# A gated linear attention and an MLP in one kernel: from a scheduler's order to a hand-written two-phase pipeline with head pairs, casting DMAs and a crossbar transpose

## The chip, the core and the metric

The kernel runs on one core of a Trainium2 chip. The core has TensorE (PE, matmuls, with its own weight loads, PEld), VectorE (DVE), ScalarE (ACT), GpSimd (POOL) and SyncE (SP). DMAs are issued here by POOL and by SP and run on 16 DMA engines. The metric is the device time of one execution, in microseconds.

## What is computed

```python
def _attn_ref(q, k, v, alpha):                 # all (4, 8, 768, 48) float32
    state = zeros((B, H, D, D)); y = zeros_like(q)
    for t in range(S):
        state = alpha[:, :, t, :, None] * state + einsum('bhd,bhe->bhde', k[:, :, t], v[:, :, t])
        y[:, :, t] = einsum('bhd,bhde->bhe', q[:, :, t], state)
    return y
def _moe_ref(x, w_in, w_out):                  # x (3072, 384), w_in (384, 2048), w_out (2048, 384)
    return gelu_tanh(x @ w_in) @ w_out
x = attn.transpose(0, 2, 1, 3).reshape(B * S, H * D)   # the heads side by side
```

Both kernels cut the 768 steps into 6 chunks of 128. Inside a chunk the decay is carried by cumulative sums of ln(alpha): with b = exp(cumulative sum), q is multiplied by b and k by 1/b, so that the chunk becomes plain attention with a mask, q' k'^T masked times v, plus q' times the state of the chunk before. The state then is (state + k'^T v) times the decay of the whole chunk. The 24 units (6 chunks x 4 batch elements) of 128 rows go through the MLP in groups of the four units of a chunk.

## The kernel before, in words

A framework schedules the program: the code below is written unit by unit, and the order on each engine is chosen by the framework from tile pools and dependences.

Front. For pairs of units alpha is loaded by POOL (L105), ln is taken on ACT (L108), and PE sums it along the rows with an upper triangular matrix (L114) and with one column sum per head (L118). DVE stores the sums (L120), and ACT takes exp of the column sums (L121). This is done for all 24 units before anything else of them. SP loads w_in (L93) and w_out (L130) as float32, and DVE casts them (L127, L159).

Rear. Three stages are staggered by one unit each. Stage a loads q, k, v (L190, POOL). Stage b takes exp of the sums with both signs (L200, L202), multiplies q and k (L205, L206), casts v (L208), transposes q and k head by head on PE (L213, L214) and copies them out of PSUM (L215 on ACT, L216 on DVE). Stage c makes the scores (L234), masks them (L237), and then y from scores and v (L241) and from q and the state (L243), and k^T v (L245); DVE updates the state (L249, L250), ACT casts y to `x_sb` (L255), PE transposes it (L259) and DVE copies it (L260).

The MLP of a group is cut into pieces: 16 of layer 1 (three matmuls L275 and a gelu L279) and 4 of layer 2 (16 matmuls L286, copy L291, store L293 on SP). Up to seven waiting pieces are put behind each stage c.

ACT has tables for sets of functions; ACT_TABLE_LOAD rows at lines L108, L121, L200, L202 and L279 are changes between them.

Of the kernel before, what the change touches and what calls it, by code (L numbers as in the profile page):

```python
# [3 lines left out]

# [6 lines left out]
BF16 = mybir.dt.bfloat16  # L12
F32 = mybir.dt.float32
AF = mybir.ActivationFunctionType
ALU = mybir.AluOpType

MU = -0.1074356


@with_exitstack  # L20
def kernel(
    ctx: ExitStack,
    tc: tile.TileContext,
    q: bass.AP,
    k: bass.AP,
    v: bass.AP,
    alpha: bass.AP,
    moe_w_in: bass.AP,
    moe_w_out: bass.AP,
    out: bass.AP,  # L30
):
    nc = tc.nc
    B, H, S, D = q.shape
    C = 128
    NCH = S // C
    NT = B * NCH
    d_model = moe_w_in.shape[0]
    d_ff = moe_w_in.shape[1]
    NKT = d_model // C
    NFT = d_ff // C  # L40

    const = ctx.enter_context(tc.tile_pool(name="const", bufs=1))
    glob = ctx.enter_context(tc.tile_pool(name="glob", bufs=1))

    ut = const.tile([C, C], BF16)
    make_upper_triangular(nc, ut, val=1.0, diag=True)
    ones_col = const.tile([C, 1], BF16)
    nc.vector.memset(ones_col, 1.0)
    iota_i = const.tile([C, 1], mybir.dt.int32)
    nc.gpsimd.iota(iota_i, pattern=[[1, 1]], base=1, channel_multiplier=1)  # L50
    bias_pos = const.tile([C, 1], F32)
    nc.vector.tensor_single_scalar(bias_pos, iota_i, MU, op=ALU.mult)
    bias_neg = const.tile([C, 1], F32)
    nc.vector.tensor_single_scalar(bias_neg, iota_i, -MU, op=ALU.mult)
    bias_end = const.tile([C, 1], F32)
    nc.vector.memset(bias_end, C * MU)
    mu_row_i = const.tile([1, C], mybir.dt.int32)
    nc.gpsimd.iota(mu_row_i, pattern=[[1, C]], base=1, channel_multiplier=0)
    mu_row = const.tile([1, C], BF16)
    nc.vector.tensor_single_scalar(mu_row, mu_row_i, MU, op=ALU.mult)  # L60
    ones_row = const.tile([1, H * D], BF16)
    nc.vector.memset(ones_row, 1.0)

    xT_all = glob.tile([C, NKT, NT, C], BF16)
    states = []
    for b in range(B):
        st = glob.tile([C, H, D], BF16, name=f"state_b{b}")
        nc.vector.memset(st, 0.0)
        states.append(st)
    cum_all = glob.tile([C, NT, H * D], mybir.dt.float16)  # L70
    bend_all = glob.tile([D, NT, H], F32)
    w_in_sb = glob.tile([C, NKT, d_ff], BF16)
    w_out_sb = glob.tile([C, NFT, d_model], BF16)
    NRING = 4
    qp_ring = [glob.tile([C, H, 64], BF16, name=f"qp_ring{i}") for i in range(NRING)]
    kp_ring = [glob.tile([C, H, 64], BF16, name=f"kp_ring{i}") for i in range(NRING)]
    for t_ in qp_ring + kp_ring:
        nc.gpsimd.memset(t_[:, :, D:64], 0.0)
    qT_ring = [glob.tile([C, H, C], BF16, name=f"qT_ring{i}") for i in range(NRING)]
    kT_ring = [glob.tile([C, H, C], BF16, name=f"kT_ring{i}") for i in range(NRING)]  # L80
    for t_ in qT_ring + kT_ring:
        nc.vector.memset(t_[64:, :, :], 0.0)
    ident = const.tile([C, C], BF16)
    from concourse.masks import make_identity
    make_identity(nc, ident)

    units = [(c, b) for c in range(NCH) for b in range(B)]

    if True:
        wstage = ctx.enter_context(tc.tile_pool(name="wstage", bufs=1))  # L90
        w_in_f32 = wstage.tile([C, NKT, d_ff], F32, tag="stage")
        for j in range(NKT):
            nc.sync.dma_start(  # L93
                w_in_f32[:, j, :], moe_w_in.rearrange("(j c) n -> c j n", c=C)[:, j, :]
            )

        psb = ctx.enter_context(tc.tile_pool(name="psb", bufs=1, space=bass.MemoryType.PSUM))
        with tc.tile_pool(name="wka", bufs=int(os.environ.get("GLA_WKA_BUFS", 5))) as wka:
            for pi in range(0, len(units), 2):
                pair = units[pi:pi + 2]  # L100
                NP2 = len(pair)
                a8 = wka.tile([C, NP2, H, D], F32, tag="a8")
                for i, (c, b) in enumerate(pair):
                    tsl = slice(c * C, (c + 1) * C)
                    nc.gpsimd.dma_start(  # L105
                        a8[:, i], alpha[b].rearrange("h s d -> s h d")[tsl])
                la8 = wka.tile([C, NP2, H, D], BF16, tag="la8")
                nc.scalar.activation(la8, a8, AF.Ln, scale=float(math.exp(-MU)))  # L108
                tts = [b * NCH + c for (c, b) in pair]
                for i, (c, b) in enumerate(pair):  # L110
                    tt = tts[i]
                    bank = psb.tile([C, H * D + H], F32, tag="hT", bufs=int(os.environ.get("MOE_HT_BUFS", 2)), name="cumla")
                    cumla, ce_i = bank[:, 0:H * D], bank[0:D, H * D:]
                    nc.tensor.matmul(cumla, ut,  # L114
                                     la8[:, i].rearrange("t h d -> t (h d)"),
                                     start=True, stop=True)
                    for h in range(H):
                        nc.tensor.matmul(ce_i[:, h:h + 1], la8[:, i, h, :],  # L118
                                         ones_col, start=True, stop=True)
                    nc.vector.tensor_copy(cum_all[:, tt, :], cumla)  # L120
                    nc.scalar.activation(bend_all[:, tt, :], ce_i, AF.Exp,  # L121
                                         bias=bias_end[0:D, 0:1], scale=1.0)

        w_out_f32 = wstage.tile([C, NFT, d_model], F32, tag="stage")
        for piece in range(8):
            psl = slice(piece * (d_ff // 8), (piece + 1) * (d_ff // 8))
            nc.vector.tensor_copy(w_in_sb[:, :, psl], w_in_f32[:, :, psl])  # L127
        for j in range(4):
            sl = slice(j * (NFT // 4), (j + 1) * (NFT // 4))
            nc.sync.dma_start(  # L130
                w_out_f32[:, sl, :],
                moe_w_out.rearrange("(n c) p -> c n p", c=C)[:, sl, :],
            )

    work = ctx.enter_context(
        tc.tile_pool(name="work", bufs=int(os.environ.get("GLA_WORK_BUFS", 4))))
    trans = ctx.enter_context(
        tc.tile_pool(name="trans", bufs=int(os.environ.get("GLA_TRANS_BUFS", 3))))
    moe = ctx.enter_context(tc.tile_pool(name="moe", bufs=2))
    args = dict(B=B, H=H, S=S, D=D, C=C, NCH=NCH, NKT=NKT, NFT=NFT,  # L140
                d_model=d_model, d_ff=d_ff, NT=NT)
    live = {}
    NU = len(units)
    GRP = B
    pending = []
    for step in range(NU + 2):
        if step < NU:
            live[step] = _gla_stage_a(nc, work, q, k, v, units[step], **args)
        if 1 <= step <= NU:
            u = step - 1  # L150
            _gla_stage_b(nc, work, trans, psb, ident, live[u], units[u],
                         cum_all, bias_pos, bias_neg,
                         qp_ring[u % NRING], kp_ring[u % NRING],
                         qT_ring[u % NRING], kT_ring[u % NRING], **args)
            if u < 4:
                for piece in (2 * u, 2 * u + 1):
                    psl = slice(piece * (NFT // 8) * d_model,
                                (piece + 1) * (NFT // 8) * d_model)
                    nc.vector.tensor_copy(  # L159
                        w_out_sb.rearrange("c n p -> c (n p)")[:, psl],  # L160
                        w_out_f32.rearrange("c n p -> c (n p)")[:, psl],
                    )
        if 2 <= step:
            u = step - 2
            c, b = units[u]
            _gla_stage_c(nc, work, psb, ident, live.pop(u), units[u],
                         ut, bend_all, states[b], xT_all, **args)
            if not int(os.environ.get("GLA_SEQ_MOE", 0)):
                take = min(int(os.environ.get("MOE_PIECES", 7)),
                           max(0, len(pending) - int(os.environ.get("MOE_RESERVE", 0))))  # L170
                for _ in range(take):
                    pending.pop(0)()
# [6 lines left out]
    while pending:  # L179
        pending.pop(0)()  # L180
# [150 lines left out]
```

## Time and profile before

| | us |
|---|---|
| median of 3 runs (lowest, highest) | 298.85 (297.84, 299.3) |
| span of the profiled execution, first to last instruction | 295.8 |
| of the median outside this span | 3.05 |
| PE / ACT / DVE / POOL busy in the span | 224.5 / 200.8 / 141.3 / 87.4 |
| PE busy in 0 to 74 us, 74 to 122, 122 to 296 | 21.0, 40.6, 162.9 |

The profile gives no other time of the profiled execution than its span; what lies around it is taken from the runs. Busy times of engines overlap, so they do not add to the span. The last line is the one to start from: PE is nearly idle in the first quarter and nearly full in the rest.

### The profile page before, as it was taken

What the parts mean: (1) busy time and instruction counts of PE and PEld (TensorE: products, weight loads), DVE (VectorE), ACT (ScalarE), POOL (GpSimd) and SP (SyncE); (2) the same over time, 40 slices, a digit from 0 to 9 for tenths busy, and PEclk for the clock granted to TensorE, in tenths of its full rate; (3) what the DMA queues carried; (4) which work ended last, traced back from release to release, by engine and by line L of the source; (5) the groups of instructions that cost most, each with busy time, mean ns of one, the idle gap of its engine ahead of it and who ended that gap; (6) DMA issues with size and microseconds to landing.
All of it is one profiled execution on the core that took longest, in us unless ns stands there. A gap on an engine that the chain in (4) does not pass through costs nothing.

```text
span 295.8 us, 5241 instructions
## 1 busy us (share of the span) xinstructions
PE 224.5 (76%) x2112; PEld 132.8 (45%) x2112; DVE 141.3 (48%) x274; ACT 200.8 (68%) x301; POOL 87.4 (30%) x114
## 2 busy tenths in 40 slices
PE   0043333332778989899998999999999999999983
PEld 0022212221656535556556555565456644554441
DVE  7183433222599855567548144656243633540011
ACT  0257787978677999996999999945761276304800
POOL 9643321005988758153333213220000000000000
PEclk9999999999999999999999999999999999999999
DMA  7999951002999979373232512241001100011011
GB/s 278 283 187 274 291 126 53 0 1 67 193 187 187 189 144 198 89 181 99 80 82 59 182 53 55 53 109 53 2 1 55 53 2 0 3 53 55 0 53 54
DMA packets 12168, 30.22 MB, mean 102 GB/s; under 512 B 2032, under 2 KB 7152, under 8 KB 11760
## 3 DMA queue, kind: packets, MB, share of 16 engines
q0 software_dynamic: 6144, 18.88, 30.4%
q1 hardware_dynamic: 6000, 11.01, 11.0%
q8 instruction: 16, 0.26, 0.4%
q14 instruction: 8, 0.07, 0.1%
HBM read 25.17 MB, written 4.72 MB: 101 GB/s over the span
## 4 chain that ended last, share of the span: by engine, by line
PE 47%; ACT 34%; DMA 7%; DVE 6%; issue 3%; POOL 1%; SPq 0%; DVEq 0%; POOLq 0%; ACTq 0%
PE acc L286 16%; PE hT L275 15%; ACT gT L279 6%; ACT L279 5%; ACT L108 4%; DMA w_in_f<-in_moe_w_in_dram 4%; ACT qT_ring L215 3%; PE kT_ps L214 3%; PE qT_ps L213 3%; ACT la L108 3%; PE at_ps L234 2%; ACT L200 2%; ACT L202 2%; ACT L121 2%; DVE w_in_sb L127 2%
## 5 line engine op out<-in xcount | busy, mean ns | idle before, releaser
L275 PE MATMUL hT<-xT_all,w_in_sb 128*128 128x512 bf16 x288 | 74.5, 379 | 4.0 <-ACT gT L279 3.8
L286 PE MATMUL acc<-w_out_sb,gT 128*128 128x384 bf16 x384 | 70.8, 326 | 3.0 <-DVE ot L291 2.8
L279 ACT ACTIVATE gT<-hT 128x512 bf16<-128x512 f32 x96 | 55.5, 598 | 16.3 <-PE hT L275 14.2
L286 PEld LDWEIGHTS <-gT 128*128 128x128 bf16 x384 | 36.4, 97 | 28.0 <-issue 4.0
L114 PE MATMUL cumla<-la,ut 128*128 128x384 bf16 x24 | 11.6, 485 | 48.3 <-ACT la L108 39.1
L291 DVE COPY ot<-acc 128x384 f32<-128x384 f32 x24 | 13.3, 555 | 53.6 <-PE acc L286 53.6
L237 DVE TENSOR_TENSOR atm<-at_ps,ut 128x512 bf16<-128x512 f32 x48 | 31.1, 683 | 15.9 <-PE at_ps L234 15.7
L275 PEld LDWEIGHTS <-w_in_sb 128*128 128x128 bf16 x288 | 24.8, 97 | 26.3 <-issue 5.5
L118 PEld LDWEIGHTS <-la 128*48 128x48 bf16 x192 | 9.5, 129 | 55.5 <-issue 55.5
L190 POOL DMA_DIRECT2D q<-in_q_dram x24 | 21.2, 884 | 44.1 <-PE cumla L118 24.1
L120 DVE CAST cum_all<-cumla 128x384 f16<-128x384 f32 x24 | 13.3, 556 | 32.5 <-PE cumla L118 32.5
L190 POOL DMA_DIRECT2D v<-in_v_dram x24 | 21.2, 885 | 25.3 <-ACT v8b L208 21.8
L105 POOL DMA_DIRECT2D a<-in_alpha_dram x24 | 21.5, 900 | 21.3 <-ACT la L108 18.9
L215 ACT COPY qT_ring<-qT_ps 64x1024 bf16<-64x1024 bf16 x24 | 24.1, 1005 | 4.9 <-PE qT_ps L213 4.6
L190 POOL DMA_DIRECT2D k<-in_k_dram x24 | 21.2, 885 | 18.3 <-DVE kp_ring L206 17.4
L208 ACT CAST v8b<-v 128x384 bf16<-128x384 f32 x24 | 12.3, 512 | 18.7 <-PE yps L243 17.9
L216 DVE COPY kT_ring<-kT_ps 64x1024 bf16<-64x1024 bf16 x24 | 16.3, 680 | 17.5 <-PE kT_ps L214 17.1
L108 ACT ACT_TABLE_LOAD x11 | 14.1, 1283 | 13.4 <-DMA a<-in_alpha_dram 13.2
L213 PE MATMUL qT_ps<-ident,qp_ring 128*64 128x128 bf16 x192 | 18.3, 230 | 5.9 <-DVE qp_ring L205 5.3
L205 DVE TENSOR_TENSOR qp_ring<-q,b 128x384 bf16<-128x384 f32 x24 | 13.2, 551 | 14.6 <-PE at_ps L234 5.7
L213 PEld LDWEIGHTS <-qp_ring 128*64 128x64 bf16 x192 | 12.7, 114 | 16.5 <-issue 14.9
L255 ACT CAST x_sb<-yps 128x384 bf16<-128x384 f32 x24 | 11.4, 476 | 12.7 <-PE yps L243 10.6
(49 smaller groups left out, 319.2 us busy)
## 6 DMA issues: line engine op xcount, KB each, us to landing
a<-in_alpha_dram POOLq DMA_DIRECT2D x24, 192.0 KB, 7.2
q<-in_q_dram POOLq DMA_DIRECT2D x24, 192.0 KB, 5.3
k<-in_k_dram POOLq DMA_DIRECT2D x24, 192.0 KB, 5.7
v<-in_v_dram POOLq DMA_DIRECT2D x24, 192.0 KB, 5.2
out_dram<-ot SPq DMA_DIRECT2D x24, 192.0 KB, 1.9
w_in_f<-in_moe_w_in_dram SPq DMA_DIRECT2D x3, 1024.0 KB, 7.4
w_out_f<-in_moe_w_out_dram SPq DMA_DIRECT2D x4, 768.0 KB, 12.4
```

Of the source, the lines that this page charges most:

```text
L105: nc.gpsimd.dma_start(a8[:, i], alpha[b].rearrange("h s d -> s h d")[tsl])
L108: nc.scalar.activation(la8, a8, AF.Ln, scale=float(math.exp(-MU)))
L120: nc.vector.tensor_copy(cum_all[:, tt, :], cumla)
L190: nc.gpsimd.dma_start(t_sb, t_dram[b].rearrange("h s d -> s h d")[tsl])
L213: nc.tensor.transpose(qT_ps[:, h, :], qp[:, h, :], ident)
L215: nc.scalar.copy(qT[0:64], qT_ps)
L216: nc.vector.tensor_copy(kT[0:64], kT_ps)
L237: nc.vector.tensor_tensor(atm, at_ps, ut[:, None, :].to_broadcast([C, 4, C]), op=ALU.mult)
L275: nc.tensor.matmul(hT, w_in_sb[:, j, nt * C:(nt + 1) * C], xsl, start=(j == 0), stop=(j == NKT - 1),)
L279: nc.scalar.activation(gT[:, nt, :], hT, AF.Gelu_apprx_tanh)
L286: nc.tensor.matmul(acc, gT[:, nt, mt * C:(mt + 1) * C], w_out_sb[:, nt, :], start=(nt == 0), stop=(nt == NFT - 1),)
L291: nc.vector.tensor_copy(ot, acc)
```

## The change

The program is written anew, under a manual order: each engine runs its instructions in the order in which the code issues them.

- Heads are kept in pairs, padded from 48 to 64 columns each, so that a pair is 128 wide. q and k are transposed on PE a pair at a time. The scores of the two heads of a pair are matmuls on 64 rows each, on the upper and the lower half of the array, into two PSUM banks. kv and the state are made for a pair at once; the state tile is zero off the diagonal blocks.
- The state has two tiles per batch element, used in turn; in chunk 0 there is no state term, in the last chunk no kv.
- ln and exp use one table set, which is loaded by hand, and there is no stored cumulative sum: exp is taken from PSUM in the phase before the unit is used.
- Two phases per group. Layer 2 of the group before runs with, merged into it, the kv and y of this group's units and ln, sums and exp of the next group. Layer 1 of this group runs with the transposes and scores of the next group.
- v, w_in and w_out are cast to bf16 by the DMA, all on POOL's queue. q, k and alpha of chunks 0 and 1 are loaded by SP, those of later chunks by POOL.
- x goes from ACT's cast to `xT` by a DMA transpose on SP's queue, where the stores are too.

```diff
-                nc.gpsimd.dma_start(a8[:, i], alpha[b].rearrange("h s d -> s h d")[tsl])
-    for t_dram, t_sb in ((q, q8), (k, k8), (v, v8)):
-        nc.gpsimd.dma_start(t_sb, t_dram[b].rearrange("h s d -> s h d")[tsl])
+    def load(self, names, pair, eng):
+        for n in names:
+            dt = F32 if n != "v" else BF16
+            t = self.ld.tile([self.C, 2, self.H, self.D], dt, tag=n + "8", bufs=6 if n == "v" else 4, name=n + "8")
...
+                e = eng if n != "v" else self.nc.gpsimd
+                e.dma_start(t[:, i], self.src[n][b].rearrange("h s d -> s h d")[sl])
...
+            ps = self.ps.tile([C, 2, H // 2, C], BF16, tag="yk", bufs=2, name="qkT_ps")
+            for j, s in enumerate((u["qp"], u["kp"])):
+                for p in range(H // 2):
+                    nc.tensor.transpose(
+                        ps[:, j, p, :], s[:, 2 * p:2 * p + 2, :].rearrange("t h d -> t (h d)"), self.ident)
+            nc.vector.tensor_copy(t, ps)
...
+        at = self.ps.tile([C, 2, H // 2, C], F32, tag="ca", name="at")
+        for p in range(H // 2):
+            for o in range(2):
+                sl = slice(64 * o, 64 * o + 64)
+                nc.tensor.matmul(at[:, o, p, :], kT[sl, p, :], qT[sl, p, :], start=True, stop=True)
...
+        x = self.wk.tile([C, H * D], BF16, tag="x", name="x")
+        nc.scalar.copy(x, yps.rearrange("t h d -> t (h d)"))
+        if DMA_X:
+            nc.sync.dma_start_transpose(xT[:, :, i, :], x)
...
+        for p in pairs[0]:
+            self.load("aqk", p, nc.sync)
...
+        for p in pairs[1]:
+            self.load("a", p, nc.sync)
+        for i in range(4):
+            self.load_w_in(i, 4)
+        for p in pairs[1]:
+            self.load("qk", p, nc.sync)
+            self.load("v", p, nc.gpsimd)
...
+                if g + 2 < len(G):
+                    side.append(lambda: [self.load("aqkv", p, nc.gpsimd) for p in pairs[g + 2]])
+                ln, cum, exp = decays(pairs[g + 1])
+                side += [lambda: self.act_set(LN_EXP_SET), ln[0]]
+                side += [lambda: self.yk(G[g][0], xT, 0), ln[1]]
+                side += [lambda: self.yk(G[g][1], xT, 1), cum[0], exp[0]]
+                side += [lambda: self.yk(G[g][2], xT, 2)]
+                side += [lambda: self.yk(G[g][3], xT, 3), cum[1], exp[1]]
...
+            main = self.layer2(G[g - 1], gT_prev) if g else []
+            _merge(main, side, 0.0, 0.8)
...
+                    side.append(lambda cb=cb: self.attn(cb))
+            _merge(self.layer1(xT, gT), side, 0.1, 1.0)
```

`_merge` spreads the side items evenly over the stated part of the main pieces; layer 1 has 16 pieces of three matmuls, layer 2 has 16 of four.

Where instructions stand. First DVE in the rear of the kernel before (`qp_ring`, `kp_ring` are q and k after the decay, `kT_ring` the transposed k):

```order
L206 TENSOR_TENSOR kp_ring_100<-k_817,binv_908 128x8x48
L237 TENSOR_TENSOR atm<-at_ps,ut 128x512 x2
L216 COPY kT_ring_116<-kT_ps 64x1024
L249 TENSOR_TENSOR stmp<-kv,state_b_83 48x384
L205 TENSOR_TENSOR qp_ring_97<-q_901,b_1026 128x8x48
L250 TENSOR_TENSOR state_b_83<-stmp,bend_all 48x384
L206 TENSOR_TENSOR kp_ring_101<-k_902,binv_1027 128x8x48
L260 COPY xT_all<-xT_ps 128x3x128
```

Then DVE now, from the states of chunk 0 to the first scores of chunk 1 (`q_166`, `k_169` are chunk 1's first pair of units, `q_175`, `k_178` its second; `qkT` is transposed q and k):

```order
L202 TENSOR_TENSOR st_1_94<-kv,bend 64x4x48 x2
L145 TENSOR_TENSOR qp_105<-q_166,b_394 128x16x48
L147 TENSOR_TENSOR kp_109<-k_169,binv_395 128x16x48
L202 TENSOR_TENSOR st_1_96<-kv,bend 64x4x48 x2
L202 TENSOR_TENSOR st_1_98<-kv,bend 64x4x48 x2
L145 TENSOR_TENSOR qp_106<-q_175,b_451 128x16x48
L147 TENSOR_TENSOR kp_110<-k_178,binv_452 128x16x48
L166 COPY qkT<-qkT_ps 128x1024
L180 TENSOR_TENSOR atm<-at,ut 128x512 x2
```

Before, units were staggered singly and each product stood near the work of its own unit; now both products of chunk 1 stand ahead of the first copy that layer 1's merged score matmuls need, with the state updates of chunk 0 between them.

SP before, all of it:

```order
L93 DMA w_in_f_135<-in_moe_w_in_dram 128x2048 x3
L130 DMA w_out_f_494<-in_moe_w_out_dram 128x4x384 x4
L293 DMA out_dram<-ot 128x384 x24
```

SP now, its start (`a_112` to `k_127` are chunk 0, `a_156` to `k_178` chunk 1):

```order
L93 DMA q_124<-in_q_dram 128x8x48 x2
L93 DMA k_127<-in_k_dram 128x8x48 x2
L93 DMA a_156<-in_alpha_dram 128x8x48 x2
L93 DMA a_159<-in_alpha_dram 128x8x48 x2
L93 DMA q_166<-in_q_dram 128x8x48 x2
L93 DMA k_169<-in_k_dram 128x8x48 x2
L93 DMA q_175<-in_q_dram 128x8x48 x2
L93 DMA k_178<-in_k_dram 128x8x48 x2
L221 DMA_TRANSPOSE xT<-x 128x3x128 x4
L258 DMA out_dram<-ot 128x384
```

POOL now, the same time (`v_172`, `v_181` are chunk 1, `a_318` to `v_339` chunk 2, `a_642` chunk 3):

```order
L100 DMA w_in<-in_moe_w_in_dram 128x3x512 x4
L93 DMA v_172<-in_v_dram 128x8x48 x2
L93 DMA v_181<-in_v_dram 128x8x48 x2
L93 DMA a_318<-in_alpha_dram 128x8x48 x2
L93 DMA q_321<-in_q_dram 128x8x48 x2
L93 DMA k_336<-in_k_dram 128x8x48 x2
L93 DMA v_339<-in_v_dram 128x8x48 x2
L106 DMA w_out<-in_moe_w_out_dram 128x4x384 x4
L93 DMA a_642<-in_alpha_dram 128x8x48 x2
```

SP had the weights and the stores; now it has 24 loads of a, q and k, then transposes and stores. POOL had all loads of a, q, k, v; now it has the weights among them.

## Rows read from the trace of the kernel before

**Rows 1.** The page, busy time and share of the span, PE
```profile
PE 224.5 (76%) x2112; PEld 132.8 (45%) x2112; DVE 141.3 (48%) x274; ACT 200.8 (68%) x301; POOL 87.4 (30%) x114
```

**Rows 2.** Busy us (count) of PE, PEld, DVE, ACT, POOL; clock, DMA share, GB/s
```profile
0.00:74.00 74.00, 21.04 (x216) 12.03 (x216) 29.15 (x59) 48.32 (x66) 28.03 (x47) 1.00 0.59 156
...
122.00:296.00 174.00, 162.87 (x1403) 93.77 (x1402) 76.23 (x146) 110.79 (x171) 23.85 (x27) 1.00 0.20 59
```

**Rows 3.** Chain of waits, the front: start us, us, what
```profile
1.65 11.86 DMA w_in_f<-in_moe_w_in_dram
13.64 6.05 DVE w_in_sb L127 x8
20.93 1.28 ACT L108
...
72.55 4.38 DMA q<-in_q_dram
```

**Rows 4.** Chain of waits, dense pieces of the rear
```profile
156.18 0.56 PE qT_ps L213 x8
...
196.62 2.60 PE acc L286 x16
...
278.20 1.33 PE hT L275 x6
```

**Rows 5.** Timeline of PE: start us, us, engine, line, operation, tiles, count
```profile
15.83 0.48 PE L118 MATMUL cumla<-ones_col,la 128*48 128x1 bf16 x8
16.24 0.50 PE L114 MATMUL cumla<-la,ut 128*128 128x384 bf16 x1
...
155.29 0.20 PE L241 MATMUL yps<-v8b,atm 128*128 128x48 bf16 x1
...
155.69 0.18 PE L243 MATMUL yps<-state_b,qT_ring 128*128 128x48 bf16 x1
```

**Rows 6.** Busy time where only w_in, w_out, and q, k, v move
```profile
3.00:6.00 3.00, 0.00 (x0) 0.00 (x0) 2.62 (x9) 0.00 (x0) 2.99 (x5) 1.00 1.02 418
25.80:27.40 1.60, 0.62 (x9) 0.50 (x9) 0.93 (x2) 1.18 (x2) 0.00 (x0) 1.00 1.07 373
86.00:96.00 10.00, 7.74 (x123) 6.07 (x124) 9.73 (x21) 7.24 (x13) 8.39 (x11) 1.00 1.05 189
```

**Rows 7.** Tiles out_dram, then w_out_f: issue to landing
```profile
DMA to landing us min/median/max: 1.8/1.9/5.0
...
DMA to landing us min/median/max: 7.8/12.4/17.0
```

**Rows 8.** The page, DMA queues: POOL's, SP's
```profile
q0 software_dynamic: 6144, 18.88, 30.4%
q1 hardware_dynamic: 6000, 11.01, 11.0%
```

**Rows 9.** Groups by line and shape: busy us, mean ns | idle before
```profile
L279 ACT ACTIVATE gT<-hT 128x512 bf16<-128x512 f32 x96 | 55.5, 598 | 16.3 <-PE hT L275 14.2
L237 DVE TENSOR_TENSOR atm<-at_ps,ut 128x512 bf16<-128x512 f32 x48 | 31.1, 683 | 15.9 <-PE at_ps L234 15.7
L279 ACT ACT_TABLE_LOAD x14 | 18.0, 1283 | 0.3
L216 DVE COPY kT_ring<-kT_ps 64x1024 bf16<-64x1024 bf16 x24 | 16.3, 680 | 17.5 <-PE kT_ps L214 17.1
...
L205 DVE TENSOR_TENSOR qp_ring<-q,b 128x384 bf16<-128x384 f32 x24 | 13.2, 551 | 14.6 <-PE at_ps L234 5.7 <-DMA q<-in_q_dram 5.2 <-PE qT_ps L213 1.1
...
L250 DVE TENSOR_TENSOR state_b<-stmp,bend_all 48x384 bf16<-48x384 f32 x24 | 13.1, 544 | 1.1 <-PE yps L243 1.0
...
L255 ACT CAST x_sb<-yps 128x384 bf16<-128x384 f32 x24 | 11.4, 476 | 12.7 <-PE yps L243 10.6 <-PE hT L275 2.0
L108 ACT ACTIVATE la<-a 128x768 bf16<-128x768 f32 x12 | 10.0, 841 | 0.1
...
L202 ACT ACT_TABLE_LOAD x6 | 7.7, 1283 | 0.1
```

**Rows 10.** Chain of waits, its last piece
```profile
292.07 0.56 DVE ot L291
```

More of the change, by code (lines that the diff above doesn't have):

```diff
@@ L2 @@
-import math
-import os
-from contextlib import ExitStack
 import concourse.bass as bass
@@ L8 @@
 from concourse import mybir
-from concourse._compat import with_exitstack
-from concourse.masks import make_upper_triangular
+from concourse.masks import make_identity, make_upper_triangular
 BF16 = mybir.dt.bfloat16
+F16 = mybir.dt.float16
 F32 = mybir.dt.float32
@@ L15 @@
 ALU = mybir.AluOpType
[L17 to L172, printed above, removed]
-            if u % GRP == GRP - 1:
-                tts = [units[uu][1] * NCH + units[uu][0]
-                       for uu in range(u - GRP + 1, u + 1)]
-                pending.extend(
-                    _moe_pieces(nc, moe, psb, xT_all, w_in_sb, w_out_sb, out,
-                                tts, **args))
-    while pending:
-        pending.pop(0)()
@@ L220, in _gla_stage_c @@
-def _gla_stage_c(nc, work, psb, ident, live, unit, ut, bend_all, state, xT_all,
-                 *, H, D, C, NCH, NKT, **_):
-    c, b = unit
-    tt = b * NCH + c
-    qT, kT, kp, v8b = live["qT"], live["kT"], live["kp"], live["v8b"]
-    yps = psb.tile([C, H, D], F32, tag="ybank",
-                   bufs=int(os.environ.get("GLA_Y_BUFS", 1)))
-    kv = psb.tile([D, H, D], F32, tag="kv", bufs=1)
-    for half in range(2):
-        at_ps = psb.tile([C, 4, C], F32, tag="at",
-                         bufs=int(os.environ.get("GLA_AT_BUFS", 2)))
-        for hh in range(4):
-            h = half * 4 + hh
-            nc.tensor.matmul(at_ps[:, hh, :], kT[:, h, :], qT[:, h, :],
-                             start=True, stop=True)
-        atm = work.tile([C, 4, C], BF16, tag="atm")
-        nc.vector.tensor_tensor(atm, at_ps, ut[:, None, :].to_broadcast([C, 4, C]),
-                                op=ALU.mult)
-        for hh in range(4):
-            h = half * 4 + hh
-            nc.tensor.matmul(yps[:, h, :], atm[:, hh, :], v8b[:, h, :],
-                             start=True, stop=False)
-            nc.tensor.matmul(yps[:, h, :], qT[:, h, :], state[:, h, :],
-                             start=False, stop=True)
-            nc.tensor.matmul(kv[:, h, :], kp[:, h, 0:D], v8b[:, h, :],
-                             start=True, stop=True)
-    stmp = work.tile([D, H, D], F32, tag="stmp")
-    nc.vector.tensor_tensor(stmp, kv, state[0:D], op=ALU.add)
-    nc.vector.tensor_tensor(
-        state[0:D], stmp, bend_all[:, tt, :, None].to_broadcast([D, H, D]),
-        op=ALU.mult)
-    x_sb = work.tile([C, H * D], BF16, tag="x_sb")
-    nc.scalar.copy(x_sb, yps.rearrange("t h d -> t (h d)"))
-    xT_ps = psb.tile([C, NKT, C], BF16, tag="ybank",
-                     bufs=int(os.environ.get("GLA_Y_BUFS", 1)))
-    for j in range(NKT):
-        nc.tensor.transpose(xT_ps[:, j, :], x_sb[:, j * C:(j + 1) * C], ident)
-    nc.vector.tensor_copy(xT_all[:, :, tt, :], xT_ps)
@@ new lines, with kernel, _merge @@
+LN_EXP_SET = 6
+DMA_QK = False
+DMA_X = True
+def kernel(tc, q, k, v, alpha, moe_w_in, moe_w_out, out):
+    from contextlib import ExitStack
+    with ExitStack() as ctx, tc.manual_schedule():
+        _Kernel(ctx, tc, q, k, v, alpha, moe_w_in, moe_w_out, out).run()
+def _merge(main, side, first=0.0, last=1.0):
+    n, m = len(main), len(side)
+    lo, hi = first * n, last * n
+    at = [lo + (hi - lo) * (i + 0.5) / m for i in range(m)] if m else []
+    j = 0
+    for i in range(n):
+        while j < m and at[j] <= i:
+            side[j]()
+            j += 1
+        main[i]()
+    while j < m:
+        side[j]()
+        j += 1
```

288 lines of the change are left out of this document (224 added, 64 removed).

## The prediction

> **What bounds the kernel now.** I read the busy line of the page first [rows 1]: the TensorE (PE) is busy 76% of the span, ScalarE (ACT) 68%, and neither is a bound over the whole. Then the busy time in three stretches [rows 2]. Up to 74 us PE works 21 us; from 122 us on it works 162.9 of 174. So there are two kernels here: a front in which the decays are made, and a rear that is bound by PE. The clock is granted in full (1.00, the level of 2.4 GHz) in both, so no term below is for the clock. The chain of waits tells what sets the front [rows 3]: the load of w_in and its cast, then pairs of an ACT table load of 1.28 us and a piece of decay work, then the first load of q, at 72.6 us. The table loads are 49 in all in five groups, the largest and the smallest shown, 1.283 us each, 62.9 us of ACT [rows 9]. In the rear the chain runs along layer 2 (16 matmuls in 2.60 us, 0.163 each), layer 1 (6 in 1.33 us, 0.222 each), transposes and score matmuls (8 in 0.56 us) [rows 4]. After the last `ot` copy come 3.8 us to the end of the span [rows 10].
>
> **The sum is made on the span**, 295.8 us; the median of the runs shown is 298.85, so 3.05 us lie around it, and I add these at the end.
>
> **The rear: what goes and what comes, on PE.** Eight heads become four pairs. Of a unit (one chunk of one batch element) 16 transposes of q and k become 8, three transposes of x go to the DMA crossbar, 8 state matmuls and 8 kv matmuls become 4 and 4 of double width, and 8 decay column sums become 4. The dear matmuls, 288 of layer 1 and 384 of layer 2, stay. With the durations of before:
> - layer 1 of a group: 48 x 0.222 = 10.7 us; layer 2: 64 x 0.163 = 10.4 us;
> - beside layer 1 stand four times 8 transposes (0.56) and 8 score matmuls. These are row-tiled, two on different halves of the array. As before they cost 0.55 us, as true pairs 0.28. I take the middle: 4 x (0.56 + 0.40) = 3.8. Layer 1 stage: 14.5 us;
> - beside layer 2 stand four times kv and y. The 48-column matmuls follow each other by 0.025 us (first and last of 16 in [rows 5]); for 96 columns no row exists, bounds are 0.025 and 0.07 (128 columns), I take 0.045: 8 x 0.045 + 8 x 0.025 = 0.56. The cumulative sum is 0.163 + 4 x 0.05 = 0.36 per unit (8 column sums in 0.41 us, [rows 5]). Layer 2 stage: 10.4 + 4 x 0.92 = 14.1 us.
>
> A small matmul takes 0.18 us from start to end though the next starts 0.025 us later [rows 5], so emptying the array costs about 0.16 us. The Trainium skill (TensorEngine Tiling (Array Packing), Key Properties) says that changing the tiling mode drains TensorE; two changes per unit would be 48 x 0.16 = 7.7 us against the 6.5 us which pairing saves, that is, 1 us worse than no pairing and some 4 us worse than my middle. No run here shows a mode change.
>
> ACT and VectorE (DVE) stay below PE. ACT in one pair of stages: 16 gelu x 0.598, two table loads, two ln of 0.84, four exp of as many elements (0.84 too), two small ones, four casts of 0.48 = about 20 us of 28.6 [rows 9]; table loads fall from 49 to 11. DVE: 8 masks x 0.683, 4 copies of 0.68, 4 products of at most twice 0.551, 16 state operations on half the columns (0.544 before, 0.35 assumed), 4 `ot` of 0.56 = 20.4 us [rows 9, 10]. This work hides under PE. The cast of v, of w_in and of w_out goes into the DMAs.
>
> What could show between the stages is the crossbar: layer 1 of a group needs x of all four units. After the last y, PE still has 5 of 16 pieces of layer 2 and a cumulative sum, 3.6 us (2.6 us in the last group). In this time run the cast (0.48) and the transpose. No row shows a crossbar transpose. The nearest is a store by the same queue, 1.8 us at least and 5.0 us at most, when POOL's loads stood beside it [rows 7]; so the wait is between nothing and 2.1 us (3.1 in the last). Loads run beside three of five of these; I take 1.5 x 5 = 7.5 us.
>
> **The front: what now ends last.** The decay phase goes; only chunk 0 and chunk 1 are needed to start. But all loads are issued at once, and the DVE order shows a place where everything meets: the product for chunk 1's second pair (`qp_106`, `kp_110`) stands ahead of the copy of the first transposed q and k of chunk 1. That copy releases the score matmuls that are merged into layer 1 of chunk 0, and PE runs in order. So PE gets through that stage only when the last of SP's 24 loads (`k_178`) has landed. How much must move until then?
> - SP: 24 loads of 196,608 bytes; POOL: 8 of v and, ahead of w_out, 16 for chunk 2. These 48 are 9.44 MB in runs of 192 bytes. Such loads alone moved 189 GB/s, with the engines full (share 1.05, third line of [rows 6]): 49.9 us.
> - w_in and w_out, 6.29 MB in long rows, moved 418 and 373 GB/s (the first two lines of [rows 6]): 15.9 us. That they are cast on the way is not in any row; reading the same bytes is taken to bound it.
> - four loads for chunk 3, freed by the first pair of chunk 1: 4.2 us.
> - SP sends a packet per run, POOL some 16 runs in one. POOL's packets took 30.4% x 16 x 295.8 / 6144 = 234 ns for 3 KB, 14.6 ns a run. SP's took 11.0% x 16 x 295.8 / 6000 = 87 ns for 1.8 KB [rows 8]; of this some 70 ns are bytes at the full rate of 418 GB/s, so 17 ns may be fixed, and a run of 192 bytes would take 24 ns. On 24 x 1024 / 16 = 1536 packets an engine this is 0 to 14 us; I take 6. The far end, a packet of 192 bytes as dear as one of 1.8 KB, is a rival below.
>
> With 1.7 us to the first bytes [rows 3] `k_178` lands at 77.7 us. That SP's small loads really come last is read from rows: SP's store took 1.8 us alone and 5.0 us beside POOL's loads, and the w_out loads 7.8 to 17.0 us where 768 KB at 373 GB/s are 2.1 [rows 7]. A queue of small packets is held up by one of large packets. The Trainium skill (DMA: Bandwidth & Descriptors, Queues, rings and completion order) states that an engine takes the queues in turn, a whole packet each; the rows agree. By it SP gets 192 bytes for each 3 to 4 KB of POOL, which gives the order assumed here; with an even split of bytes the first rival holds.
>
> Then 3 us (product, copy, and what is left to start layer 1), and 10.7 us of the 14.5 of the first layer 1 stage.
>
> **Sum:** 77.7 + 3 + 10.7 + 4 x (14.1 + 14.5) + (10.4 + 4 x 0.56) + 10.7 + 10.4 + 3.8 + 7.5 = 250.8 us of span; with 3.05 around it 254 us. The rear gives the gain: the old one, from the landing of the first q at 76.9 us to the end, is 219 us, the new one, from 77.7 on, 173. The front ends where it ended.
>
> **Rivals.**
> 1. The queues share by bytes. Then beside SP's 4.72 MB only as much of POOL's goes: v and w_in. 6.29 MB of runs at 189 GB/s and 3.15 MB at 418, with 1.7 and 6: 48.5 us, 29 us sooner, 225 us. For it: the trace of before never had runs of 192 bytes on both queues, and rows 7 tell of sharing with SP's packets of 1.5 KB only. Against it: these too were held up.
> 2. The crossbar is slow or is held up. If a transpose lands 10 us after the cast (w_out took up to 17.0 in the same crowd), the five waits become 7 us each: 254 - 7.5 + 35 = 281 us. For it: transposes share SP's queue with stores that wait for `ot`, and loads run in just these stages. Against it: a unit's x is 96 KB, half of a store, and four are spread over the stage. At 10.5 us of wait each nothing would be gained.
> 3. Slower: SP's one-run packets cost nearly what SP's packets cost in rows 8. At 68 ns instead of 14.6 plus my 4, the 1536 packets add 76 us to the front: 330 us. It decides from about 48 ns a packet (45 us more), where the front alone eats what the rear gains. For it: no row shows a small packet on that queue, and the packet may have a price of its own. Against it: a packet of 1.8 KB would then be nearly free of charge for its bytes.
>
> **Chances.** Forecast 0.55 (its own range 240 to 270 us); rival 1 0.18; rival 2 0.15; rival 3 0.12. The range of 8 in 10 reaches from 230 (half of rival 1 is outside) to 294 (rival 3 is outside). A change of 0.5% is about what a measurement of this kernel can tell from none. Faster by more than that: 0.55 + 0.18 + nearly all of rival 2 = 0.86; within it 0.02; slower 0.12.
>
> **What would show it.** Right: the first dense PE stretch begins near 75 us; just before it PE waits at the score matmuls for the DVE copy, DVE for `kp`, and that for a load on SP; from then on layer 1 and layer 2 stages of about 14 us each with PE above 90%; 11 table loads; SP's loads take far longer to land than POOL's. Wrong: PE dense from 45 to 50 us on (rival 1); PE idle for several us ahead of each layer 1, with layer 1 released by a DMA into `xT` (rival 2); the front longer than 110 us with POOL's queue empty and SP's still full (rival 3). A score stage of over 1 us a unit would show that pairing drains more than it saves.

## The result and the profile after

The changed kernel took 259.0 us (median of 4 runs, 257.13 to 260.2) against 298.72 us (4 runs) of the kernel before: ratio 0.866, 95% interval 0.862 to 0.870. 254 us were forecast. The profiled execution took 257.13 us and its span is 255.3 us, so 1.8 us lie around it and not the 3.05 that were added. Of the kernel of experiment 1 with x on TensorE only one of four runs was undisturbed (260.6 us; the others took 265.5 to 267.3 us at a lower clock), and its trace is of a disturbed one: its time is that one run's, and from its trace the order of things and the front are read, not the total.

The page, answering to [rows 1] and [rows 8]: busy time, DMA queues, and the chain that ended last by engine.

```profile
PE 174.9 (69%) x1517; PEld 101.7 (40%) x1528; DVE 109.2 (43%) x201; ACT 111.0 (43%) x179; POOL 74.1 (29%) x102
...
q0 software_dynamic: 31744, 14.95, 44.7%
q1 hardware_dynamic: 38400, 11.80, 26.4%
...
PE 55%; SPq 26%; DMA 8%; DVE 6%; issue 2%; ACT 0%; DVEq 0%; ACTq 0%
```

PE lost 49.6 us of work and ACT 89.8. POOL's queue (q0) now takes 5 times the packets for fewer bytes: 24 x 1024 = 24576 of them are as many as the casting loads of v have runs, so v's runs, some 16 to a packet before, go one to a packet now. And 26% of the chain is SP's queue, a thing that the chain before did not have. Where it stands is seen in the chain's front (start us, us, what), answering to [rows 3]:

```profile
54.95 7.57 SPq L93
...
67.00 1.51 SPq L93
...
68.62 5.45 DMA xT<-x
...
74.67 5.02 DMA xT<-x
...
79.83 0.59 PE hT L236
...
80.63 3.19 PE hT L236 x7
```

L93 on SP are the loads. The dense part begins at 79.83 us (76.9 forecast), and what it waits for is the crossbar (`xT<-x`), which waits for SP. SP's own timeline, and what DVE, PE and ACT did then (in brackets the idle time before, and who ended it):

```profile
62.56 5.95 SPq L93 DMA_DIRECT2D k<-in_k_dram  x2
68.62 7.23 SPq L221 DMA_TRANSPOSE xT<-x  x4
```

```profile
67.23 0.96 DVE L147 TENSOR_TENSOR kp<-k,binv 128x768 bf16<-128x768 f32 x1 [12.91 <-DMA k<-in_k_dram]
68.21 1.48 DVE L202 TENSOR_TENSOR st<-kv,bend 64x192 bf16<-64x192 f32 x4
...
68.99 0.48 PE L216 MATMUL yps<-v,atm 128*128 128x48 bf16 x8 [18.00 <-DVE st L202]
```

```profile
74.17 0.48 ACT L219 CAST x<-yps 128x384 bf16<-128x384 f32 x1 [23.71 <-DMA xT<-x]
```

Three things end within 2 us of each other: SP is through with its 24 loads (68.5 us), so the transposes can start at all; chunk 1's first k lands (67.1), so DVE gets past `kp` to the states of chunk 0 that stand behind it; and y of unit 3, for which PE had waited 18 us, is made. Then the fourth cast waits for the first transpose, because x has three buffers.

Busy time in two stretches (us; PE, PEld, DVE, ACT, POOL; clock, DMA share, GB/s), answering to [rows 2]:

```profile
0.00:80.00 80.00, 13.40 (x153) 9.78 (x154) 19.80 (x37) 14.81 (x23) 43.96 (x68) 1.00 1.34 173
80.00:252.00 172.00, 161.54 (x1365) 91.89 (x1374) 88.87 (x164) 96.14 (x156) 30.15 (x35) 0.99 0.44 75
```

Again a front and a rear: the front is now full of transfers (share 1.34, 173 GB/s) and nearly empty of work. The rear, from the chain of waits, answering to [rows 4], and what PE waited for in all:

```profile
117.27 0.33 PE at L177 x8
...
122.47 1.29 PE hT L236 x6
...
127.57 2.54 PE acc L251 x15
```

```profile
PE hT L236 <- DMA xT<-x: 14.4, 3, 9.5
...
PE yps L213 <- DVE stmp L200: 3.6, 4, 1.4
```

Six matmuls of layer 1 and 16 of layer 2 last as before. Eight paired scores go in 0.33 us, where 0.28 to 0.55 were the bounds.

| | forecast us | measured us |
|---|---|---|
| layer 1 of chunk 0 starts | 76.9 | 79.8 |
| that stage | 14.5 | 16.2 |
| four pairs of stages | 114.4 | 117.6 |
| waits for xT behind the first | 7.5 | 4.9 |
| last layer 2 with y, layer 1, layer 2 | 33.7 | 33.4 |
| tail | 3.8 | 3.3 |
| span | 250.8 | 255.3 |

ACT has 11 table loads, as forecast. The four pairs are 79.83 + 16.24 to 218.57 us (start of the last layer 2 with y) less the 4.9 us of waits.

### The profile page after: what moved, and what is told of

Its sections match the earlier page's. It is cut to its first block, busy times and chain, and to the rows that moved or that the text cites. A ratio compares the mean times of both kernels' runs of the same rounds, so it can differ in the third digit from the quotient of the medians.

```text
span 255.3 us, 3848 instructions
## 1 busy us (share of the span) xinstructions
PE 174.9 (69%) x1517; PEld 101.7 (40%) x1528; DVE 109.2 (43%) x201; ACT 111.0 (43%) x179; POOL 74.1 (29%) x102
## 3 DMA queue, kind: packets, MB, share of 16 engines
q1 hardware_dynamic: 38400, 11.80, 26.4%
## 4 chain that ended last, share of the span: by engine, by line
PE 55%; SPq 26%; DMA 8%; DVE 6%; issue 2%; ACT 0%; DVEq 0%; ACTq 0%
SPq L93 26%; PE hT L236 25%; PE acc L251 20%; DMA xT<-x 8%; PE qkT_ps L164 4%; PE at L177 3%; DVE qp L145 2%; DVE qkT L166 1%; DVE kp L147 1%; PE yps L213 1%; PE yps L216 1%; DVE stmp L200 1%; PE cum L128 1%; DVE st L202 1%; PE kv L191 1%
## 5 line engine op out<-in xcount | busy, mean ns | idle before, releaser
L236 PE MATMUL hT<-xT,w_in 128*128 128x512 bf16 x277 | 71.5, 393 | 15.6 <-DMA xT<-x 14.4
L251 PE MATMUL acc<-w_out,gT 128*128 128x384 bf16 x384 | 67.9, 326 | 0.0
L236 PEld LDWEIGHTS <-w_in 128*128 128x128 bf16 x288 | 26.5, 100 | 43.9 <-issue 13.4
L180 DVE TENSOR_TENSOR atm<-at,ut 128x512 bf16<-128x512 f32 x48 | 30.9, 686 | 18.9 <-PE at L177 18.9
L219 ACT CAST x<-yps 128x384 bf16<-128x384 f32 x24 | 11.5, 478 | 48.5 <-DMA xT<-x 23.7
L166 DVE COPY qkT<-qkT_ps 128x1024 bf16<-128x1024 bf16 x24 | 16.6, 691 | 31.4 <-PE qkT_ps L164 31.4
L145 DVE TENSOR_TENSOR qp<-q,b 128x768 bf16<-128x768 f32 x12 | 11.5, 958 | 35.7 <-ACT b L141 18.6
L93 POOL DMA_DIRECT2D a<-in_alpha_dram x16 | 14.4, 910 | 34.3 <-ACT la L120 30.0
L93 POOL DMA_DIRECT2D v<-in_v_dram x24 | 21.5, 913 | 5.3 <-DMA v<-in_v_dram 4.5
L164 PE MATMUL qkT_ps<-ident,qp 128*128 128x128 bf16 x96 | 10.7, 242 | 14.8 <-DVE qp L145 14.8
L93 POOL DMA_DIRECT2D q<-in_q_dram x16 | 14.2, 901 | 17.5 <-DVE qp L145 13.8
L93 POOL DMA_DIRECT2D k<-in_k_dram x16 | 14.2, 901 | 15.5 <-DVE kp L147 12.4
L147 DVE TENSOR_TENSOR kp<-k,binv 128x768 bf16<-128x768 f32 x12 | 11.4, 952 | 16.7 <-DMA k<-in_k_dram 16.7
L177 PE MATMUL at<-qkT 64*128 64x128 bf16 x192 | 10.4, 233 | 4.9 <-DVE atm L180 4.2
```

The costliest lines, as they stand in the source:

```text
L93: e.dma_start(t[:, i], self.src[n][b].rearrange("h s d -> s h d")[sl])
L145: nc.vector.tensor_tensor(qp[:, :, :, 0:D], u0["qpair"], b8.rearrange("t i (h d) -> t i h d", h=H), op=ALU.mult)
L147: nc.vector.tensor_tensor(kp[:, :, :, 0:D], u0["kpair"], binv8.rearrange("t i (h d) -> t i h d", h=H), op=ALU.mult)
L164: nc.tensor.transpose(ps[:, j, p, :], s[:, 2 * p:2 * p + 2, :].rearrange("t h d -> t (h d)"), self.ident)
L166: nc.vector.tensor_copy(t, ps)
L177: nc.tensor.matmul(at[:, o, p, :], kT[sl, p, :], qT[sl, p, :], start=True, stop=True)
```

## Experiments

**1. x on TensorE; four buffers of x.** Theory A: the crossbar behind SP's loads ends the front. Theory B: the loads end it, through DVE's order, as forecast.

```diff
-DMA_X = True
+DMA_X = False                                  # first kernel
-        x = self.wk.tile([C, H * D], BF16, tag="x", name="x")
+        x = self.wk.tile([C, H * D], BF16, tag="x", bufs=4, name="x")    # second kernel
```

> x is transposed on TensorE and copied by VectorE, as before the change; everything else as changed. Theory A (in the front the crossbar transposes stand on SP's queue behind the loads of chunk 1, and two of them, 5.45 and 5.02 us, are in series on the chain): layer 1 of chunk 0 starts near 71 us instead of 79.8, the two later waits of 2.6 and about 2.5 us for xT go, and 20 units x 0.2 us of transposes come back on TensorE: about 250 us, ratio to before 0.837. Theory B (the front ends when all loads have moved, whatever the transposes do): layer 1 starts at 77 us or later and the time is 259 to 262 us.

> One more buffer for ScalarE's cast of x (4 instead of 3). Theory A: the cast of the fourth unit no longer waits for the first transpose to land; the last transpose is issued 3.6 us after the first, at 72.2 us, and lands near 77: 2 to 3 us sooner, 256 to 257 us. Theory B: nothing, 259 us. A third reading, that crossbar transposes run one after the other at 4 to 5 us each, gives nothing either, with four landings spread over 16 us.

Without the crossbar 260.6 us (one run), with four buffers 259.39 (ratio 0.865, 0.859 to 0.871): no gain in either. The chain of the first kernel:

```profile
65.07 13.67 DMA k<-in_k_dram
...
78.87 0.96 DVE kp L147
79.83 0.61 DVE qkT L166
...
80.49 0.61 PE at L177 x6
...
93.13 2.71 PE acc L251 x16
```

That is the forecast's mechanism link by link: the last k of chunk 1, the product, the copy, the scores. With the crossbar gone it binds. But the equal times hide a gain and a loss, as the first kernel's layer 1 and PE's waits show:

```profile
L236 PE MATMUL hT<-xT,w_in x288: 379/379/634, 67.1 to 251.4; 128*128 128x512 bf16 x144
```

```profile
PE xT_ps L225 <- ACT x L219: 19.2, 24, 2.8
...
PE at L177 <- DVE qkT L166: 7.2, 1, 7.2
```

Layer 1 of chunk 0 starts at 67.1 us in this trace, sooner than either theory had it (79.8 with the crossbar); then PE stands 7.2 us at the scores, and the stage ends at 93.1 us in place of 96.1. So A names what ended the front. What the front gains is lost in the rear, where PE now waits for the cast of x: a pair of stages takes 32.5 us (111.87 to 144.34) against 29.4 (175.20 to 204.58) in the changed kernel; experiment 3 has the 32.5 again. In the second kernel the cast no longer waits, but the transposes take as long:

```profile
69.67 4.43 SPq L221
...
76.78 5.07 DMA xT<-x
```

**2. Which loads hold up which.** In the first kernel POOL's loads of w_out and chunk 2 wait for `k_178`; in the second chunk 1's a, q and k go by POOL, so that SP is free for the transposes. In the first w_out also goes ahead of chunk 2.

```diff
-                side.append(lambda: [self.load_w_out(i, 4) for i in range(4)])
+                def late():                                   # first kernel
+                    t = self.wk.tile([self.C, 1], F32, tag="gate", name="gate")
+                    nc.gpsimd.tensor_copy(t, self.u[pairs[1][1][0]]["kpair"][:, 1, 0, 0:1])
+                    for i in range(4):
+                        self.load_w_out(i, 4)
+                    for p in pairs[2]:
+                        self.load("aqkv", p, nc.gpsimd)
+                side.insert(0, late)
...
-            self.load("qk", p, nc.sync)
+            self.load("qk", p, nc.gpsimd)                     # second kernel (and "a")
```

> POOL's w_out and chunk 2 loads wait, by a copy of one column on POOL, until chunk 1's last load on SP has landed; w_out is put ahead of chunk 2. Theory A (an engine takes one packet of each queue in turn, so each 192-byte packet of SP waits for a packet of POOL): SP's packets then cost 15 ns each where POOL is quiet; the last SP load lands near 40 us, layer 1 of chunk 0 starts near 50, and the total is 228 to 232 us. Theory B (bytes): 9.4 MB at 170 GB/s until then, 55 us, layer 1 at 66, 245 us.

> Chunk 1's loads of alpha, q and k go on POOL's queue, where some 21 runs share a packet, behind w_in and ahead of chunk 2; SP keeps chunk 0's twelve loads. Theory A: SP's 768 packets an engine are through near 25 us and the transposes find the queue empty; chunk 1 lands near 42 us, layer 1 of chunk 0 starts near 46 us, total 225 to 230 us. Theory B (bytes alone, 9.4 MB at 170 GB/s, 55 us): layer 1 near 62 us, 242 us. If one-run packets had a price of their own on SP's queue, this would gain the most of the four.

Held back, 236.47 us (ratio 0.790, 0.789 to 0.792); chunk 1 on POOL, 246.22 (0.819, 0.816 to 0.823). Both gain much, by moving no byte less. But the first lies between its theories and the second above both; the chains say why, first the one with the loads held back, then chunk 1 on POOL:

```profile
45.82 7.91 DMA xT<-x
...
53.86 4.00 PE hT L236 x9
```

```profile
47.23 11.56 DMA xT<-x
...
59.40 7.92 DMA xT<-x
...
67.45 2.72 PE hT L236 x6
```

SP's last loads, of the first and of the second kernel:

```profile
37.94 3.17 SPq L93 DMA_DIRECT2D k<-in_k_dram  x2
```

```profile
11.47 6.92 SPq L93 DMA_DIRECT2D k<-in_k_dram  x2
```

In the first they are all issued by 41.1 us (68.5 after). In the second SP had issued its last load by 18.4 us, and yet a transpose takes 8 to 12 us: it is not the place on SP's queue alone, the transposes themselves are held up beside POOL's loads. So are SP's own: chunk 0's last k lets DVE go on only at 36.8 us (28.6 in the changed kernel), where theory A had all of SP's loads through near 25.

**3. What is left when the loads are held back.** Four variants on the first kernel of experiment 2: x on TensorE; chunk 2's loads held until the fourth transpose has landed; the scores in another order; x on TensorE and w_in held back too, until chunk 0's last k has landed.

```diff
+                    nc.gpsimd.tensor_copy(t, xT[:, 0, 3, 0:1])      # second: ahead of chunk 2's loads
-        for p in range(H // 2):
-            for o in range(2):
+        for o in range(2):                                          # third
+            for p in range(H // 2):
...
+        nc.gpsimd.tensor_copy(t, self.u[pairs[0][1][0]]["kpair"][:, 1, 0, 0:1])   # fourth: ahead of w_in
```

> As the gated kernel (POOL's loads of w_out and of chunk 2 wait for k_178's landing), and x transposed on TensorE with a DVE copy in place of the crossbar. Theory A, what is left of the front and of the gaps in the gated kernel is the crossbar itself, whose transposes took 7.9 to 9.1 us beside POOL's loads: layer 1 of chunk 0 starts at 45 to 47 us (53.9 gated) and the two or three later waits for xT, 17 us in all with the first, shrink to under 1 us a group; against it stand some 60 short transposes and 20 copies, about 0.5 us a group. Total 218 to 222 us against 236.5. Theory B, the loads end the front with or without the crossbar, as they did when it was taken out of the ungated kernel: only the later waits go, total 228 to 232 us.

> As the gated kernel with the crossbar kept, and POOL's loads of chunk 2 wait until the fourth transpose of x of chunk 0 has landed, so that the first transposes run beside w_out's tail at most. Theory A, it is POOL's packets beside them that make the transposes slow: the last front transpose takes 2.3 to 4.4 us in place of 7.9, layer 1 of chunk 0 starts at 49 to 51 us in place of 53.9, total 232 to 234 us if chunk 2 is still in time. Theory B, a transpose is slow by itself in this place: start at 53 to 54 us, total 236 us.

> As the gated kernel, with the score matmuls of a unit issued four on the upper half of the array and then four on the lower, in place of one above and one below in turn; nothing else differs. Theory A, two matmuls on different halves overlap and that is why eight of them took 0.33 us: now they take 0.55 us, 20 units x 0.22 us = 4.4 us more, 241 us in place of 236.5. Theory B, eight such matmuls take 0.33 us in any order, or the order costs a change of mode each time: the time stays at 236 to 237 us or falls.

> As gated with x on TensorE, and w_in too waits, until the last k of chunk 0 (k_127) has landed. Theory A, POOL's large packets hold SP's 192-byte packets up in the whole front: chunk 0 lands some 6 us sooner, layer 1 of chunk 0 starts at 38 to 42 us, total 212 to 216 us. Theory B, w_in then lands too late itself, or the sum of bytes decides and not their order: layer 1 starts at 46 us or later, total as gated with x on TensorE, 218 to 222 us, or more.

Measured: 238.54 (ratio 0.796, 0.793 to 0.800), 236.76 (0.792, 0.789 to 0.795), 237.23 (0.792, 0.788 to 0.795), 234.0 (0.784, 0.781 to 0.787). The first lies above both of its theories and the fourth far above its theory A; the second and the third lie near their theories B.

The first came out no faster than the kernel with the crossbar (236.47; one of its runs, 236.85, lies among that kernel's), and slower than both theories allowed. Layer 1 did start sooner, at 48.4 us; but a pair of stages rose from 28.9 us to 32.5, and the wait stood in a new place (its waits of PE, from the last kernel of the four):

```profile
PE xT_ps L225 <- ACT x L219: 16.9, 24, 1.4
```

PE runs in order, so at each of 24 units it waits for the cast ahead of the transposes. The second tells nothing apart: w_out moved beside the first transposes, which took up to 7.8 us again. The third says that the order of the scores is free: eight take 0.34 us against 0.33. The single records show two starting 3 ns apart in one order and 13 ns in the other, and the next two some 55 ns later in both; they do not name the half of the array that a matmul ran on. So matmuls overlap in twos either way, and this experiment did not undo the pairing. The fourth (chain, then DVE, then PE):

```profile
28.35 10.89 DMA k<-in_k_dram
```

```profile
39.36 0.96 DVE L147 TENSOR_TENSOR kp<-k,binv 128x768 bf16<-128x768 f32 x1 [3.09 <-DMA k<-in_k_dram]
```

```profile
41.01 0.48 PE L191 MATMUL kv<-v,kp 128*128 128x96 bf16 x4 [4.03 <-DVE st L202]
```

Layer 1 starts at 43.7 us; DVE's order, chunk 1's product ahead of chunk 0's states, costs PE 4 us here.

**4. Crossbar without loads beside it; transposes later; products later.** All three on the fourth kernel of experiment 3. First: the crossbar again for chunks 3 to 5. Second: x on TensorE, a piece or more of layer 2 behind the cast. Third: as the first, with the products of a chunk's first pair behind the states of units 2 and 3.

```diff
-        if DMA_X:
+        if c >= 3:                                                            # first, third
...
-                side += [lambda: self.yk(G[g][0], xT, 0), ln[1]]
+                side += [lambda: self.yk(G[g][0], xT, 0), ln[1], lambda: self.xt(xT, 0)]     # second
...
-                side += [lambda: self.yk(G[g][3], xT, 3), cum[1], exp[1]]
+                side += [lambda: self.yk(G[g][3], xT, 3), lambda: self.e_mul(pairs[g + 1][0])]   # third
+                side += [cum[1], exp[1], lambda: self.e_mul(pairs[g + 1][1])]
```

> As the kernel in which both weights wait for the last k of their chunk and x is transposed on TensorE (234.0 us), but with the crossbar again for x of chunks 3, 4 and 5, where no loads are left to run beside. Theory A, the crossbar is dear beside loads only, and without them it is the cheaper way: a pair of stages took 28.9 us with it (from 125.39 to 154.30 us in the gated kernel) and 32.5 us with x on TensorE (from 83.32 to 115.79 us), so three chunks gain 3 x 3.6 = 10.8 us: 222 to 224 us. Theory B, the difference of the two pairs came from the loads' places and not from x: 232 to 235 us.

> As the kernel in which both weights wait for the last k of their chunk and x is transposed on TensorE in all chunks (234.0 us), but each unit's three transposes of x are issued at least one piece of layer 2 (0.65 us) later, so that PE has work while ACT casts x. Theory A, the dear part of transposing on PE is PE's wait for the cast (0.49 us of ACT and some 0.4 us around it per unit, PE in order), not the transposes: of 3.6 us a pair of stages 2 to 3 come back, 5 x 2 to 3 us, total 219 to 224 us. Theory B, the transposes and their copies are the price: 231 to 235 us.

> As the kernel with the crossbar for chunks 3 to 5 alone, and DVE's products qp and kp of the next chunk's first pair stand behind the state operations of units 2 and 3 in place of ahead of them. Theory A, the wait of PE for stmp in each layer 2 stage (0.75 us, at 150.00 us in the gated kernel, and 0.15 to 0.3 us at the kv of that unit) is DVE's order alone: five stages x 0.8 to 1.2 us, 4 to 6 us below the other kernel of this call. Theory B, the products then come late for the next layer 1's first transposes of q and k, and what the one stage gains the other loses: no difference.

Measured: 222.9 us (ratio 0.746, 0.744 to 0.749), 224.34 (0.752, 0.748 to 0.757), 221.86 (0.743, 0.740 to 0.746). In the first the twelve transposes that are left land so (tile `xT`; then the kernel of experiment 2 with all 24):

```profile
DMA to landing us min/median/max: 2.3/2.3/3.0
```

```profile
DMA to landing us min/median/max: 2.3/3.4/14.1
```

So the crossbar is not slow, it is slow beside loads; alone it is the cheaper way by some 3.6 us a pair (11.1 us in three chunks), as theory A said. The second shows that more than half of those 3.6 us were PE's wait for the cast: 9.7 us came back by order alone (1.9 us for each of five pairs), and PE's wait for the cast fell from 16.9 us to the last line here. In its place stand waits for DVE's copies of the transposed x:

```profile
PE yps L213 <- DVE xT L230: 5.5, 5, 1.3
PE hT L239 <- DVE xT L230: 4.5, 5, 2.5
...
PE xT_ps L229 <- ACT x L219: 1.2, 2, 0.6
```

The third gained 1.0 us (222.9 to 221.86), between its theories. Its layer 1 starts at 39.9 us instead of 44.1, and a later pair of stages takes 28.4 us instead of 29.5, but the gain in front is lost again in waiting for chunk 2's loads, where PE once stands still for 4.8 us (2.1 in the first kernel). The chain:

```profile
48.85 9.29 DMA q<-in_q_dram
58.15 7.33 DMA a<-in_alpha_dram
```

**5. All together,** with chunk 2's v loads behind its a, q and k.

```diff
+                    for p in pairs[2]:
+                        self.load("aqk", p, nc.gpsimd)
+                    for p in pairs[2]:
+                        self.load("v", p, nc.gpsimd)
```

> What the runs so far showed, together: the weights wait for the last k of their chunk; x by the crossbar for chunks 3 to 5, on TensorE for chunks 0 to 2, there a piece or more of layer 2 behind the cast; the products for the next chunk behind the state operations; and chunk 2's v loads behind all of its a, q and k. Theory: from the kernel with the crossbar for chunks 3 to 5 and the products behind (221.9 us) the waits for the cast in two chunks (2 x 2 us, as 9.7 us for five showed) and some 2 to 4 us of waiting for chunk 2's loads go: 214 to 218 us. Rival: layer 2 of chunk 0 goes on waiting for chunk 2's loads whatever their order, and the rest is hidden there: 219 to 222 us.

214.55 us (5 runs; ratio 0.719, 0.717 to 0.721), within the theory, and the fastest of all. The chain's front, and the busy time from layer 1 on:

```profile
38.96 0.59 PE hT L245
...
55.51 8.19 DMA a<-in_alpha_dram
```

```profile
39.00:212.00 173.00, 162.32 (x1389) 92.59 (x1399) 95.66 (x176) 97.99 (x160) 59.64 (x69) 1.00 0.66 112
```

Its rear is 212.5 - 39.0 = 173.5 us against 175.5 in the changed kernel: of the 42.8 us between the two spans 40.8 are front, 79.8 to 39.0. The rival is right in part: 8.2 us of the chain are still a load of chunk 2, but PE works through most of them and stands still for 2.7 us.

## Why the prediction was right, and where it was not

- **The rear gives the gain: right.** From the first dense piece to the end 175.5 us against 173.9 forecast (its 173 are counted from 77.7 us, its layer 1 starts at 76.9), 219 before. Layer 1 stages behind the first took 14.0 to 14.2 us (14.5 forecast), one with a lower clock 15.8; the layer 2 stages without a wait for xT took 14.75 and 15.4 (14.1 forecast), with 0.75 us of a wait that was not in the sum: DVE's states of a unit stand behind the next chunk's products (the `stmp` row, 3.6 us in four stages). Putting the products behind took 1.1 us from a pair. This is shown stage by stage in one trace; which part of the change gave how much of it (pairs, casts in the DMA, fewer table loads) no run tells apart, but for the way of x.
- **The middle for the paired scores (0.40): slightly dear,** 0.33 measured. The Trainium skill (TensorEngine Tiling (Array Packing), Key Properties) says that a change of tiling mode drains TensorE, by which pairing would have been 1 us worse than none. The trace does not bear that price out: with the change to them and back, eight scores and what follows come 0.33 us after each other, less than the 0.55 of before. (Against the middle the prediction's working gives 1.2 + 24 x 0.15 = 4.8 us, where it says some 4.) A kernel with no pairing at all was not tried.
- **The front: right in size, in good part by luck.** Claimed was that PE waits at the score matmuls for `kp_110`, and that for `k_178`, landing at 77.7 us. DVE's order did hold PE, but one product earlier: `kp_109` and chunk 1's first k, with the states of chunk 0 behind them and y behind these, 18 us. `k_178` itself was issued at 67.0 us and landed after 5.2, at 72.2, 5.5 us before its forecast; `qp_106` and `kp_110` waited for ACT's exp, which stands behind the fourth cast, and not for it. From there SP's queue decided: the crossbar waits had been put into the rear alone, 5 times 1.5 us, while the first four transposes stand behind all 24 loads on SP and then take 11.2 us (68.62 to 79.83). The sum missed it. So a load that came sooner and a term that was left out went against each other, and layer 1 started at 79.8 us where 76.9 were forecast. The claimed chain exists, as x on TensorE showed: with the crossbar gone the scores start at 80.5 us, 80.7 by the sum. But there `k_178` landed at 78.7 us, 6.5 later than in the changed kernel; POOL's next loads of k had gone out 4.5 us sooner (64.3 against 68.8 us), which fits and is not shown to be the cause.
- **SP's loads come last, POOL's are served ahead: right.** Two stretches of the changed kernel, 54 to 60 us and 24 to 30 us (queue, packets, MB, share of 16 engines):

```profile
q0 software_dynamic: 1182, 0.88, 93.5%
q1 hardware_dynamic: 1181, 0.22, 33.9%
...
q0 software_dynamic: 2964, 0.30, 87.2%
q1 hardware_dynamic: 2717, 0.51, 78.5%
```

  One packet of each in turn, 1182 to 1181, and so four times the bytes for POOL (packets of 768 bytes here, w_out's, where the prediction had 3 to 4 KB). In the second stretch POOL's packets are the small ones of v, and the bytes go the other way. The Trainium skill (DMA: Bandwidth & Descriptors, Queues, rings and completion order) gives this rule, and the trace agrees (1182 packets to 1181). The sign named for it, landing times, came out weakly: from 35 to 68 us SP's loads of q and k landed 16.3 and 12.3 us after their issue, POOL's 11.3 and 9.8, because much of SP's delay stands in the issue, which for 24 loads lasts until 68.5 us. Holding POOL's later loads back gave 22.5 us (259.0 to 236.47): the forecast's rival of sharing by bytes was wrong as a rule, but its price, 29 us, is of the size of what SP's loads going first is worth.
- **Crossbar: forecast 7.5 us for the rear, 4.9 measured,** but not spread evenly: two waits beside loads and next to none without. Rival 2 (transposes held up by loads) was right as a mechanism: 5.0 to 6.0 us in front, and up to 14.1 in experiment 2. The queue rows give a reason that fits. Without the crossbar q1 has 28416 packets and 9.44 MB, with it 38400 and 11.80: a transpose is 9984 / 24 = 416 packets of 236 bytes in the mean, 26 an engine. If each waits for one of POOL's large packets, 234 ns by the prediction's working from [rows 8], that is 6.1 us on top of 2.3, an estimate of 8.4 us, where the chains of experiment 2 have 7.9 to 11.6. No run shows it packet by packet.
- **Rival 3 (small SP packets as dear as large ones) was wrong:** the front did not pass 80 us. In the kernel with the loads held back SP's queue is almost alone from 33 to 41 us, and its 7736 packets take 102.4% of 16 engines' time, 17 ns each; the sum had 18.6, this rival 68.

## What to carry to other kernels

Put the loads that work waits for first in time, not only first on their queue: two queues share the engines by packets, so a queue of short runs starves beside one of long ones, and holding the large one back by a one-column copy on its issuing engine was worth 22 us here. A crossbar transpose is such a queue of short runs: use it where no loads move, and TensorE, with other work between cast and transpose, where they do. When a change brings no difference, look at the stages before calling it free: without the crossbar the front gained and the rear lost. In a written-out order, look on each in-order engine for an instruction that waits for a transfer and stands ahead of work that doesn't need it.

## What was not expected of the hardware

- The first matmuls of layer 1 go at half pace: 7 in 3.19 us, 0.456 us each against 0.216, with a recorded clock of 1.00 in 79.8 to 83.8 us. After a wait of 2.3 us, in 144.6 to 148.6, the same is seen with a recorded clock of 0.62 (us; PE, PEld, DVE, ACT, POOL; clock, DMA share, GB/s):

```profile
79.80:83.80 4.00, 3.75 (x10) 1.53 (x12) 0.00 (x0) 1.19 (x2) 2.12 (x3) 1.00 1.45 168
...
144.60:148.60 4.00, 3.94 (x17) 2.11 (x19) 0.00 (x0) 1.79 (x3) 4.00 (x5) 0.62 1.42 243
```

  0.456 us is about twice 0.216, as at the lower of the two levels, 1.2 GHz in place of 2.4; PE had stood still for 9.5 us ahead of the first. But after a wait of 2.6 us, at 113.4, the pace and the record stayed full (7 in 1.68 us). Why the record is at 1.00 in the first is open. The slow pace costs some 1.7 us a time.
- Issued four for one half of the array and then four for the other, the score matmuls still start in twos; on which halves these ran, the records do not say.
